# The first operations of a fused attention and channel-mix kernel: inputs on other queues, w_phi in one DMA, k's first transposes ahead of q

## The chip, the cores and the metric

One core of one Trainium2 chip. The metric is the device time of one execution in microseconds (us). The kernel before took 284.57, 334.05 and 285.87 us in three runs; the median is 285.87. A profile comes from one execution, and its times count from the first instruction of the program, the start of the span.

## The reference

The input is q, k and v of shape (8, 8, 576, 64) (batch, heads, sequence, head dimension), a feature matrix `w_phi` (64 x 128), and the parameters of a channel mix. First an attention with a feature map, then the mix on its output:

```python
def phi(x):
    proj = np.einsum('bhsd,df->bhsf', x, w_phi)
    proj = proj - np.max(np.abs(proj), axis=-1, keepdims=True)
    return np.concatenate([np.exp(proj), np.exp(-proj)], axis=-1)
q_p, k_p = (phi(q), phi(k))
kv = np.einsum('bhsf,bhsd->bhfd', k_p, v)
num = np.einsum('bhsf,bhfd->bhsd', q_p, kv)
den = np.einsum('bhsf,bhf->bhs', q_p, np.sum(k_p, axis=2))[..., None] + 1e-06
x = (num / den)                      # heads side by side: (8, 576, 512)
...
xk = mu_k * x + (1.0 - mu_k) * x_prev     # x_prev: x one position earlier
xr = mu_r * x + (1.0 - mu_r) * x_prev
k = np.maximum(xk @ w_k, 0.0)
v = k * k @ w_v
out = 1.0 / (1.0 + np.exp(-(xr @ w_r))) * v
```

Inputs and the output are float32; matrix products run on bfloat16 operands.

## The kernel before

Work is cut into 32 pairs of heads (8 batches of 4 pairs). Within a pair, 128 partitions hold two heads of 64 partitions, and each partition has nine positions of 64 values: 576 columns of k, then 576 of q, in the tile `nat` (1152 columns, nine groups of 128). Groups 0 to 3 are k alone, group 4 is the last 64 columns of k and the first 64 of q, groups 5 to 8 are q alone. For the first two batches TensorE transposes these groups (`pt`, L331 to L339, with the identity `ident`), ScalarE or VectorE copies them from PSUM to the tile `qkT` (`pa` and `pb`, L341 to L347); later batches are transposed by DMA.

Per pair n the operations are, by the names that the order uses:

- `ptn.0`, `ptn.1`: two runs of transposes, and `pan`, `pbn`: their copies. `trn` is only a name for both.
- `kpn`, `qpn` (L571, L574): projections of k (groups 0 to 3) and q (groups 5 to 8) with `wph` (w_phi in bf16, on both halves of the partitions). `tp` (L457) does group 4, the odd position.
- `rkn`, `rqn` (L577, L582): VectorE's maxima of absolute values; `rt` (L470) for group 4.
- `ean`, `ebn` (L602): ScalarE's exponentials of k; `em`, `eme`, `ekt` smaller ones.
- `mh`, `mt`, `mc`, and `mhe`, `mte`, `mce` for group 4: the maxima of q are split into two bf16 parts on GpSimd, transposed and copied. `qt` and `qa`, `qb` then form the exponentials of q transposed (L626, L639).
- `va`, `vb` (L595): v scaled on GpSimd. `kv`, `kc`, `nd`, `ra`, `rd`: products, division.
- `xt`, `xe`, `xf`, `df`, `xa`, `xb`: the mix; `h`, `rl`, `sq`, `r`, `th`, `v`, `ob`, `so`: the channel mix itself.

Nothing schedules this at run time. `plan.op(...)` registers each operation as a function, and the string `ORDER` (L19) is the order in which all of them are issued, written out. In `name/ENGINE` the engine is chosen, in `name:i` the PSUM buffer, and `+n@i` puts n filler matmuls of the tile `ones` (L285) ahead of the operation; their product is not used. Each engine runs its instructions in this order, and an instruction waits for the semaphores of the tiles that it touches. The costs and dependences that `op` is given are not used by `order()`.

What starts the kernel:

- `hk` (L358) loads k of pair 0 as float32 on the SP queue, `hq` (L362) q on the ACT queue, each 128 partitions of 2304 bytes. `lk0.0.d` (VectorE) and `lq0.0.d` (ScalarE) cast them into `nat`.
- `wphi` (L244) loads w_phi in two DMAs of 64 partitions on SP; `dve1` (L251) casts it to `wph`.
- `mus` (L442) loads the mix factors `mu_k_t` and `mu_r_t` on SP, element by element.
- `lk`, `lq` (L317) load and cast the other pairs through the GpSimd (POOL) queue, `lv` (L324) loads v on POOL or SP, `wk`, `wr`, `wv` (L431) the weights on POOL.
- `ident` (L248) makes the identity on GpSimd, `ones`, `dve2`, `dve3` (L254 to L272) set constants on VectorE: zeroed tiles, a column of `xs`, ones in `tq`, the bf16 identity, and a selection matrix `sel`.

Of the kernel before, what the change touches and what calls it, by code (L numbers as in the profile page):

```python
# [16 lines left out]


ORDER = """  # L19
ones hk hq ident dve2 hk.d hq.d wphi wphi.d lk0.1 lk0.1.d lq0.1 lq0.1.d mus mus.d lk0.2 lk0.2.d dve3  # L20
lq0.2 lq0.2.d lv0.0/POOL lv0.0.d lk0.0.d/DVE lq0.0.d/ACT lv0.1/SP lv0.1.d pt0.0:0+9@0 lv0.2/SP
lv0.2.d pt0.1:1 pa0/DVE pb0/ACT tr0 dve1 tp0.0:0+1@2 kp0:1 rt0.0 qp0:2 rk0 eme0.0 mhe0.0/POOL ekt0.0
pt1.0:1+1@0 lk1.0 lk1.0.d pa1/ACT mte0.0:0 rq0 ea0 lq1.0 lq1.0.d pt1.1:1+2@2 pb1/DVE tr1 lk1.2
lk1.2.d eb0 kp1:2+2@2 tp0.1:0 lq1.2 lq1.2.d rt0.1 em0 rk1 qp1:1+1@1 ekt0.1 mh0/POOL eme0.1 wk.0
wk.0.d mt0:1+1@1 mc0/ACT mce0.0/DVE rq1 ea1 qt0:0+1@2 wk.1 wk.1.d wk.d pt2.0:1 qa0 pt2.1:0
mhe0.1/DVE mh1/POOL pa2/DVE pb2/DVE tr2 eb1 vb0/POOL pt3.0:1+2@3 pt3.1:0 pa3/DVE qb0 pb3/DVE tr3
va0/POOL mte0.1:1+1@3 qp2:2 mt1:0 rq2 qp3:1 mce0.1/ACT mc1/ACT em1 qte0.1:1 wr.0 wr.0.d qt1:0 eqe0.1
qte0.0:0 rq3 lv1.0/POOL lv1.0.d qa1 tp0.2:2 va1/POOL qb1 rt0.2 kp2:1+3@1 rk2 vb1/POOL ekt0.2
# [103 lines left out]
class Plan:  # L132
# [6 lines left out]
    def op(self, name, eng, w, at, fn, deps=(), alloc=(), rel=(), chain=None, mode=0, port=False, alt=()):  # L139
        assert name not in self.ops, name  # L140
        self.ops[name] = dict(name=name, fn=fn, alloc=alloc, alt=alt)
# [19 lines left out]
def kernel(  # L161
# [80 lines left out]
    mu_r_t = consts.tile([128, NDC], FP, name="mu_r_t")  # L242

    def c_wphi():  # L244
        for hh in range(2):
            nc.sync.dma_start(out=wph_f32[64 * hh:64 * hh + 64, :], in_=w_phi)

    def c_ident():  # L248
        make_identity(nc, ident_f32)
# [4 lines left out]
    def c_ones():  # L254
        nc.vector.memset(ones, 1.0)

    def c_dve2():
        for t in mhls + mhlts + [zero]:
            nc.vector.memset(t, 0.0)
        for t in xss:  # L260
            nc.vector.memset(t[:, :, 0:1], 0.0)
        for t in tqs[0] + tqs[1]:
            nc.vector.memset(t[:, :, 0:64], 1.0)

    def c_dve3():
        nc.vector.tensor_copy(ident, ident_f32)
        for i in range(2):
            iv = ident_f32[:, 64 * i:64 * i + 16].rearrange("p (k l g) -> p k l g", k=2, l=2)
            nc.vector.tensor_tensor(sel3[:, i, :].rearrange("p (k g) -> p k g", k=2),
                                    iv[:, :, 0, :], iv[:, :, 1, :], op=ALU.add)  # L270
        nc.vector.tensor_tensor(sel3[:, 2, :], sel3[:, 0, :], sel3[:, 1, :], op=ALU.add)
        nc.vector.tensor_copy(sel, sel3[:, 2, :].to_broadcast([128, 8, 128]))  # L272

    op("wphi", "SP", 1.2, -98, c_wphi, ["hk"])
    op("wphi.d", "DMA", 0.1, -98, None, ["wphi"])
    op("ident", "POOL", 1.1, -99, c_ident)
    op("ones", "DVE", 0.3, -10, c_ones)
    op("dve1", "DVE", 0.2, -9, c_dve1, ["wphi.d", "dve2"])
    op("dve2", "DVE", 1.9, -8, c_dve2, ["ones"])
    op("dve3", "DVE", 1.3, -7, c_dve3, ["ident", "dve2"])  # L280

    st = {}
# [29 lines left out]
    def add_load(b, a0, a1, at, first):  # L312
        al = lambda t: [(t, (t, b))] if first else []
        n = a1 - a0
        tag = f"{b}.{a0}"

        def ld(which):  # L317
            def f():
                t = get(nat, b, inp, [128, NP, 2 * X], BF, "nat")
                src, o = ((k, 0), (q, X))[which]  # L320
                nc.gpsimd.dma_start(out=t[:, a0:a1, o:o + X], in_=heads(src, b, a0, a1))
            return f

        def ldv(c0, c1):  # L324
            def f(eng):
                t = get(vt, (b, c0 // 2), inp, [128, 2, X], FP, "vt", bufs=BUFS["vt"])
                (nc.sync if eng == "SP" else nc.gpsimd).dma_start(out=t[:, c0 % 2:c0 % 2 + c1 - c0, :],
                                                                  in_=heads(v, b, c0, c1))
            return f

        def pt(b, a, bk):  # L331
            def f():
                i = NP * b + a
                get(qkT, b, inp, [128, NP * R, 128], BF, "qkT")
                ps = motile(("mo", f"pt{i}.{bk}"), "ps_pt")
                st["pb", i, bk] = pb = ps.bitcast(BF).rearrange("p (g t) -> p g t", t=128)
                for g in range(5 * bk, min(R, 5 * bk + 5)):
                    nc.tensor.transpose(pb[:, g - 5 * bk, :], nat[b][:, a, g * 128:(g + 1) * 128], ident)
            return f  # L339

        def pc(b, a, bk):  # L341
            def f(eng):
                t = qkT[b]
                n_ = 5 - bk
                o = t[:, R * a + 5 * bk:R * a + 5 * bk + n_, :]
                copy(eng, o, st["pb", NP * b + a, bk][:, 0:n_, :])
            return f  # L347

        def tr(p0, p1):
            def f():  # L350
                t = get(qkT, b, inp, [128, NP * R, 128], BF, "qkT")
                nc.sync.dma_start_transpose(out=t[:, R * p0:R * p1, :],
                                            in_=nat[b][:, p0:p1, :].rearrange("p a x -> p (a x)"))
            return f

        g = 0.95 * n
        if b == 0 and a0 == 0:
            def hk():  # L358
                st["kq"] = mm.tile([128, NFC, 512], BF, name="kk").rearrange("p a x -> p (a x)").bitcast(FP)[:, 0:2 * X].rearrange("p (i x) -> p i x", i=2)
                nc.sync.dma_start(out=st["kq"][:, 0, :], in_=heads(k, 0, 0, 1)[:, 0, :])  # L360

            def hq():  # L362
                nc.scalar.dma_start(out=st["kq"][:, 1, :], in_=heads(q, 0, 0, 1)[:, 0, :])

            def ck(i):
                def f(eng):
                    t = get(nat, b, inp, [128, NP, 2 * X], BF, "nat")
                    o = t[:, 0, i * X:(i + 1) * X]
                    copy(eng, o, st["kq"][:, i, :])
                return f  # L370

            op("hk", "SP", 0.6, -99, hk)
            op("hk.d", "DMA", g, -99, None, ["hk", "dve2"])
            op("hq", "ACT", 0.6, -99, hq, ["hk"])
            op("hq.d", "DMA", g, -99, None, ["hq", "dve2"])
            op(f"lk{tag}.d", "DVE", 0.4, -90, ck(0), ["hk.d"], alloc=al("nat"), alt=("DVE", "ACT"))
            op(f"lq{tag}.d", "ACT", 0.65, -90, ck(1), ["hq.d", f"lk{tag}.d"], alt=("ACT", "DVE"))
        else:
            op(f"lk{tag}", "POOL", 0.75, at("lk"), ld(0), ["ident"], alloc=al("nat"), chain="ld")
            op(f"lk{tag}.d", "DMA", g, at("lk"), None, [f"lk{tag}"])  # L380
            op(f"lq{tag}", "POOL", 0.75, at("lq"), ld(1), [f"lk{tag}"], chain="ld")
            op(f"lq{tag}.d", "DMA", g, at("lq"), None, [f"lq{tag}"])
        for c0 in range(a0, a1, 2):
            c1 = min(c0 + 2, a1)
            vn = f"lv{b}.{c0}"
            op(vn, "POOL", 0.75, at("lv"), ldv(c0, c1), ["ident"], chain="lv", alt=("POOL", "SP"),
               alloc=[("vt", ("vt", (b, c0 // 2)))] if c0 % 2 == 0 else [])
            op(vn + ".d", "DMA", g, at("lv"), None, [vn])
        if b < NPT:
            for a in range(a0, a1):  # L390
                i = NP * b + a
                for bk in range(2):
                    op(f"pt{i}.{bk}", "PE", 0.3, ("pt", i), pt(b, a, bk), [f"lk{tag}.d", f"lq{tag}.d", "dve3"],
                       alloc=[("mo", ("mo", f"pt{i}.{bk}"))] + (al("qkT") if a == a0 and bk == 0 else []), rel=[("nat", b)],
                       chain="pt")
                    op(f"{'pa' if bk == 0 else 'pb'}{i}", "DVE", 0.48, ("pa", i), pc(b, a, bk), [f"pt{i}.{bk}"],
                       rel=[("mo", f"pt{i}.{bk}")], alt=("DVE", "ACT"))
                op(f"tr{i}", "NONE", 0, 0, None, [f"pa{i}", f"pb{i}"])
        else:
            for p0 in range(a0, a1, 2):  # L400
                tg = f"tr{b}.{p0}"
                op(tg, "SP", 2.8, at("tr"), tr(p0, p0 + 2), [f"lk{tag}.d", f"lq{tag}.d"], chain="tr",
                   alloc=al("qkT") if p0 == a0 else [])
                op(tg + ".d", "DMA", 2, at("tr"), None, [tg], rel=[("nat", b)])
                for a in range(p0, p0 + 2):
                    op(f"tr{NP * b + a}", "NONE", 0, 0, None, [tg + ".d"])
# [35 lines left out]
    def mus():  # L442
        nc.sync.dma_start(out=mu_k_t, in_=moe_mu_k.rearrange("(c p) -> p c", p=128))
        nc.sync.dma_start(out=mu_r_t, in_=moe_mu_r.rearrange("(c p) -> p c", p=128))

    op("mus", "SP", 1.2, -3, mus, ["wphi"])
    op("mus.d", "DMA", 0.3, -3, None, ["mus"])

# [568 lines left out]
```

## Time and profile before

| | |
|---|---|
| median of three runs | 285.87 us |
| span of the profiled execution | 275.3 us |
| its records ahead of the span | 10.8 us, so about 286.1 us in all |
| first DMAs of k and q: issue to landing | 3.9 and 4.1 us |
| the two of w_phi | 3.8 and 4.4 us |
| mu_k, mu_r | 7.1 and 8.5 us |
| three parts of v of batch 0 | 8.0, 8.6 and 9.8 us |
| filler matmuls ahead of the first transposes | 9, 4.02 us |
| first transposes start | 5.53 us |
| first projection of k starts | 7.01 us |
| second pair's first exponential of k starts | 12.03 us |

How to read it: a row of the timeline gives start, duration, engine, line, operation, output<-inputs, shapes, a count when several are merged, and in brackets the idle time of the engine before it and what ended that. PE is TensorE, PEld its weight loads, DVE VectorE, ACT ScalarE, POOL GpSimd, SP the queue of SyncE; a q behind a name means the sequencer, as when it issues a DMA. An operation's reported end lies some 0.1 us behind the start of the next one on the same engine, so a chain is summed from start to start. The packet records of the trace give queue, size, start and duration of each DMA packet.

### The profile page before, as it was taken

Reading aid. Unit: us, or ns where it says so; the run is one execution under the profiler, and the core shown is the slowest. Engines: PE = TensorE matmul, PEld = TensorE weight load, DVE = VectorE, ACT = ScalarE, POOL = GpSimd, SP = SyncE. Lnnn points to the kernel's source line nnn. Section 1 sums busy time; section 2 is a strip of 40 time slices with the busy share of each in tenths; the row PEclk is TensorE's granted clock in tenths of the full one; section 3 lists DMA queues with packets and bytes.
Section 4 is the critical chain, followed back from the end, with each engine's and each line's share of the span. In section 5 each row is a group of like instructions: output and inputs, shape, how many; then the busy total and the mean of one; then the engine's idle time right before and its main releaser. Section 6 shows DMA issues by size and latency. Waiting matters only on the chain.

```text
span 275.3 us, 8865 instructions
## 1 busy us (share of the span) xinstructions
PE 261.7 (95%) x3682; PEld 154.1 (56%) x3730; DVE 234.6 (85%) x388; ACT 223.1 (81%) x413; POOL 142.4 (52%) x193
## 2 busy tenths in 40 slices
PE   7899889999899999999999999999999999999993
PEld 3567656566555566555565666555566565444542
DVE  6999999999799989999999889998889897864222
ACT  3899999999899997899898999789987777616330
POOL 5799557976818682633459465821931611300200
PEclk9999999999999999999999999999999999999999
DMA  7999999599999899759699998981725324142134
GB/s 147 285 209 250 209 213 174 114 235 175 238 129 200 202 219 185 155 127 248 99 166 164 215 249 142 171 255 41 161 89 88 77 52 100 42 110 67 29 88 116
DMA packets 65817, 42.89 MB, mean 156 GB/s; under 512 B 47152, under 2 KB 57008, under 8 KB 65776
## 3 DMA queue, kind: packets, MB, share of 16 engines
q1 hardware_dynamic: 54496, 27.54, 49.3%
q0 software_dynamic: 11056, 14.42, 29.1%
q8 instruction: 29, 0.48, 0.8%
q10 hardware_dynamic: 224, 0.36, 0.5%
q14 instruction: 12, 0.10, 0.1%
HBM read 33.62 MB, written 9.44 MB: 156 GB/s over the span
## 4 chain that ended last, share of the span: by engine, by line
PE 75%; DVE 8%; ACT 6%; issue 4%; DMA 3%; POOL 2%; SPq 0%; POOLq 0%; ACTq 0%
PE ps_h L810 19%; PE ps_v L843 17%; PE ps_r L829 9%; PE ps_nd L677 5%; PE ps_kv L656 5%; DMA qkT<-nat 3%; PE ps_he L897 3%; PE ps_ve L929 3%; PE ps_k L566 2%; PE ps_qT L630 2%; PE ps_q L566 2%; PE ps_qT L636 2%; ACT k L605 2%; DVE nmk L579 2%; PE ps_f L292 1%
## 5 line engine op out<-in xcount | busy, mean ns | idle before, releaser
L597 POOL TENSOR_TENSOR v<-vt,v 128x576 bf16<-128x576 f32 x59 | 69.8, 1203 | 33.5 <-ACT v L591 31.1
L605 ACT ACTIVATE k<-ps_k 128x1024 bf16<-128x1024 f32 x64 | 64.8, 1047 | 1.3 <-DVE nmk L579 1.3
L643 ACT ACTIVATE q<-ps_qT 128x1024 bf16<-128x1024 f32 x64 | 63.8, 1054 | 1.8 <-PE ps_qT L636 1.7
L810 PE MATMUL ps_h<-xk,wk_bf 128*128 128x512 bf16 x235 | 60.5, 380 | 1.2
L843 PE MATMUL ps_v<-wv_bf,kk 128*128 128x512 bf16 x244 | 58.2, 379 | 0.6
L579 DVE TENSOR_REDUCE nmk<-ps_k 128x8 f32<-128x1024 f32 x32 | 38.8, 1217 | 1.8 <-PE ps_k L566 1.5
L584 DVE TENSOR_REDUCE nmq<-ps_q 128x8 f32<-128x1024 f32 x32 | 38.3, 1217 | 1.6 <-PE ps_q L566 1.4
L843 PEld LDWEIGHTS <-kk 128*128 128x128 bf16 x256 | 24.1, 98 | 27.3
L810 PEld LDWEIGHTS <-wk_bf 128*128 128x128 bf16 x256 | 22.7, 97 | 25.0 <-issue 0.7
L206 ACT ACTIVATE krelu<-ps_h 128x512 bf16<-128x512 f32 x48 | 28.8, 611 | 9.3 <-PE ps_h L810 9.3
L726 POOL TENSOR_TENSOR diff<-xs 128x576 bf16<-128x576 bf16 x15 | 20.2, 1346 | 28.8 <-ACT xs L706 12.7
L214 POOL TENSOR_TENSOR kk<-krelu 128x512 bf16<-128x512 bf16 x18 | 19.1, 1068 | 30.3 <-ACT krelu L206 26.6
L849 DVE SCALAR_TENSOR_TENSOR ob<-rt,ps_v 128x512 f32<-128x512 bf16 x32 | 21.7, 682 | 14.3 <-PE ps_v L843 12.7
L829 PE MATMUL ps_r<-wr_bf,xr 128*128 128x512 bf16 x116 | 31.1, 380 | 0.7
L835 ACT ACTIVATE rt<-ps_r 128x512 bf16<-128x512 f32 x32 | 19.7, 615 | 8.8 <-PE ps_r L829 8.7
L732 DVE SCALAR_TENSOR_TENSOR xk<-diff,mu_k_t,xs 128x576 bf16<-128x576 bf16 x32 | 26.7, 839 | 0.1
L689 DVE TENSOR_TENSOR x_sc<-ps_nd,rden 128x640 bf16<-128x640 f32 x32 | 26.0, 817 | 0.6
L732 DVE SCALAR_TENSOR_TENSOR xr<-diff,mu_r_t,xs 128x576 bf16<-128x576 bf16 x32 | 25.6, 806 | 0.1
L656 PE MATMUL ps_kv<-v,k 64*128 64x65 bf16 x1024 | 22.4, 190 | 0.5 <-ACT q L643 0.2
L566 PEld LDWEIGHTS <-qkT 64*128 64x128 bf16 x512 | 16.5, 94 | 11.0 <-issue 8.0
L656 PEld LDWEIGHTS <-k 64*128 64x128 bf16 x1024 | 19.3, 94 | 5.7 <-issue 1.8
L677 PE MATMUL ps_nd<-kv,q 128*128 128x65 bf16 x512 | 21.4, 193 | 0.0
(102 smaller groups left out, 414.3 us busy)
## 6 DMA issues: line engine op xcount, KB each, us to landing
out_dram<-ob SPq DMA_DIRECT2D x70, 128.0 KB, 2.5
vt<-in_v_dram SPq DMA_DIRECT2D x11, 576.0 KB, 6.1
nat<-in_k_dram POOLq DMA_DIRECT2D x6, 576.0 KB, 7.8
nat<-in_q_dram POOLq DMA_DIRECT2D x6, 576.0 KB, 8.0
vt<-in_v_dram POOLq DMA_DIRECT2D x4, 576.0 KB, 6.0
wk_bf<-in_moe_w_k_dram POOLq DMA_DIRECT2D x2, 512.0 KB, 11.4
wv_bf<-in_moe_w_v_dram POOLq DMA_DIRECT2D x2, 512.0 KB, 10.6
nat<-in_k_dram POOLq DMA_DIRECT2D x3, 288.0 KB, 6.9
```

What stands on the lines that cost most here:

```text
L206: nc.scalar.activation(out_, in_, AF.Relu, scale=HALF)
L579: nc.vector.tensor_reduce(t[:, j, :], s["k"].rearrange("p a (g f) -> p (a g) f", f=128), axis=AX.X, op=ALU.max, apply_absolute_value=True, ...
L584: nc.vector.tensor_reduce(t[:, j, :], s["q"].rearrange("p a (g f) -> p (a g) f", f=128), axis=AX.X, op=ALU.max, apply_absolute_value=True, ...
L597: (nc.vector if eng == "DVE" else nc.gpsimd).tensor_tensor(vb[:, a, pn, :, 0:64], vt[b, a // 2][:, a % 2, :].rearrange("p (s d) -> p s d", ...
L605: nc.scalar.activation(s[f"k{pn}"], s["k"].rearrange("p a (g f) -> p (a g) f", f=128), AF.Exp, scale=(1.0 if pn == 0 else -1.0))
L643: nc.scalar.activation(t.rearrange("f x (a p) -> f x a p", a=2), s["qT"].rearrange("f a (x p) -> f x a p", p=64), AF.Exp, scale=(1.0 if pn ...
L656: nc.tensor.matmul(ps[:, hh, pn * 65:(pn + 1) * 65], lhsT=s[f"k{pn}"][r, c, :], rhs=vb[r, a, pn, 2 * g + par, :], start=(pn == 0 and c == ...
L677: nc.tensor.matmul(ps[:, bk, o * 65:(o + 1) * 65], lhsT=tail if sl < 2 else s[f"q{pn}"][:, 2 * G + h, :], rhs=s["kv"][:, h, pn, :], start= ...
L732: nc.vector.scalar_tensor_tensor(out=t[:, a, (b % 2) * S:(b % 2 + 1) * S], in0=s["d"], scalar=mu[:, a:a + 1], in1=xs[:, a, 0:S], op0=ALU.m ...
L810: nc.tensor.matmul(ps, lhsT=wk_bf[:, c, fc * 128:(fc + 1) * 128], rhs=xkt[bp][:, c, m0:m0 + 512], start=(c == 0), stop=(c == NDC - 1))
L829: nc.tensor.matmul(ps, lhsT=xrt[bp][:, c, m0 + ci * 128:m0 + (ci + 1) * 128], rhs=wr_bf[:, c, :], start=(c == 0), stop=(c == NDC - 1))
L843: nc.tensor.matmul(ps, lhsT=s["kk"][:, fc, ci * 128:(ci + 1) * 128], rhs=wv_bf[:, fc, :], start=(fc == 0), stop=(fc == NFC - 1))
```

## The change

The first operations are issued in another order and on other queues; from `wk.1` on the order is the same string as before.

- q of pair 0 is issued on SP right behind k; w_phi is one DMA on ACT, whose source is the matrix read twice.
- A pair's nine transposes are cut 4+5 instead of 5+4, for all pairs that TensorE transposes.
- The constants: the cast of the identity (`dve0`) comes first, then the zeroed tiles (`dve2`), then `dve3`; the column of `xs` and the ones in `tq` are set on GpSimd (`dve4`).
- On VectorE the cast of w_phi (`dve1`) comes ahead of the copy `pa0`; on TensorE `kp0` comes ahead of `pt0.1`, with `pt1.0`, `tp0.0` and `qp0` behind. On ScalarE: q's cast, `pb0`, `pa1`, `ea0`, `ekt0.0`, `eb0`, `eme0.0`.
- On GpSimd `mh0` comes ahead of the loads `lk1.2` and `lq1.2`. Behind these stands `muz`, which zeroes `mu_k_t`; the DMAs of the mix factors wait for it, and `lv0.2` follows them on SP. `lv0.1` moves from SP to POOL.
- Eight filler matmuls stand ahead of `wk.1` instead of 17.

```diff
-ones hk hq ident dve2 hk.d hq.d wphi wphi.d lk0.1 lk0.1.d lq0.1 lq0.1.d mus mus.d lk0.2 lk0.2.d dve3
-lq0.2 lq0.2.d lv0.0/POOL lv0.0.d lk0.0.d/DVE lq0.0.d/ACT lv0.1/SP lv0.1.d pt0.0:0+9@0 lv0.2/SP
-lv0.2.d pt0.1:1 pa0/DVE pb0/ACT tr0 dve1 tp0.0:0+1@2 kp0:1 rt0.0 qp0:2 rk0 eme0.0 mhe0.0/POOL ekt0.0
-pt1.0:1+1@0 lk1.0 lk1.0.d pa1/ACT mte0.0:0 rq0 ea0 lq1.0 lq1.0.d pt1.1:1+2@2 pb1/DVE tr1 lk1.2
-lk1.2.d eb0 kp1:2+2@2 tp0.1:0 lq1.2 lq1.2.d rt0.1 em0 rk1 qp1:1+1@1 ekt0.1 mh0/POOL eme0.1 wk.0
-wk.0.d mt0:1+1@1 mc0/ACT mce0.0/DVE rq1 ea1 qt0:0+1@2 wk.1 wk.1.d wk.d pt2.0:1 qa0 pt2.1:0
+ones hk hk.d wphi wphi.d hq hq.d ident dve0 lk0.1 lk0.1.d dve2 lq0.1 lq0.1.d lk0.2 lk0.2.d dve3
+lq0.2 lq0.2.d lv0.0/POOL lv0.0.d lv0.1/POOL lv0.1.d lk0.0.d/DVE pt0.0:0+5@0 dve4 lq0.0.d/ACT dve1
+pa0/DVE kp0:1+1@2 pt0.1:1 rk0 pb0/ACT pt1.0:0 tr0 tp0.0:0 rt0.0 qp0:2 pa1/ACT mhe0.0/POOL rq0 ea0
+pt1.1:1+1@0 lk1.0 lk1.0.d ekt0.0 pb1/DVE tr1 mte0.0:0 lq1.0 lq1.0.d kp1:2 tp0.1:0 eb0 rt0.1
+mh0/POOL eme0.0 rk1 qp1:1+1@1 lk1.2 lk1.2.d mt0:1 mc0/ACT em0 lq1.2 lq1.2.d mce0.0/DVE muz mus mus.d
+lv0.2/SP lv0.2.d rq1 ekt0.1 wk.0 wk.0.d eme0.1 ea1 qt0:0+1@2 wk.1 wk.1.d wk.d pt2.0:1 qa0 pt2.1:0
...
     def c_wphi():
-        for hh in range(2):
-            nc.sync.dma_start(out=wph_f32[64 * hh:64 * hh + 64, :], in_=w_phi)
+        twice = bass.AP(w_phi.tensor, w_phi.offset, [[0, 2]] + [list(x) for x in w_phi.ap])
+        nc.scalar.dma_start(out=wph_f32, in_=twice)
...
+    def c_dve0():
+        nc.vector.tensor_copy(ident, ident_f32)
+
     def c_dve2():
         for t in mhls + mhlts + [zero]:
             nc.vector.memset(t, 0.0)
+
+    def c_dve4():
         for t in xss:
-            nc.vector.memset(t[:, :, 0:1], 0.0)
+            nc.gpsimd.memset(t[:, :, 0:1], 0.0)
         for t in tqs[0] + tqs[1]:
-            nc.vector.memset(t[:, :, 0:64], 1.0)
+            nc.gpsimd.memset(t[:, :, 0:64], 1.0)
...
-                for g in range(5 * bk, min(R, 5 * bk + 5)):
-                    nc.tensor.transpose(pb[:, g - 5 * bk, :], nat[b][:, a, g * 128:(g + 1) * 128], ident)
+                for g in ((0, 1, 2, 3), (4, 5, 6, 7, 8))[bk]:
+                    nc.tensor.transpose(pb[:, g - 4 * bk, :], nat[b][:, a, g * 128:(g + 1) * 128], ident)
...
-                n_ = 5 - bk
-                o = t[:, R * a + 5 * bk:R * a + 5 * bk + n_, :]
+                n_ = 4 + bk
+                o = t[:, R * a + 4 * bk:R * a + 4 * bk + n_, :]
...
-                nc.scalar.dma_start(out=st["kq"][:, 1, :], in_=heads(q, 0, 0, 1)[:, 0, :])
+                nc.sync.dma_start(out=st["kq"][:, 1, :], in_=heads(q, 0, 0, 1)[:, 0, :])
...
+    def muz():
+        nc.gpsimd.memset(mu_k_t, 0.0)
+
+    op("muz", "POOL", 0.1, -3, muz)
```

More of the change, by code (lines that the diff above doesn't have):

```diff
@@ L259, in c_dve2 @@
             nc.vector.memset(t, 0.0)
+    def c_dve4():
         for t in xss:
-            nc.vector.memset(t[:, :, 0:1], 0.0)
+            nc.gpsimd.memset(t[:, :, 0:1], 0.0)
         for t in tqs[0] + tqs[1]:
-            nc.vector.memset(t[:, :, 0:64], 1.0)
+            nc.gpsimd.memset(t[:, :, 0:64], 1.0)
     def c_dve3():
-        nc.vector.tensor_copy(ident, ident_f32)
         for i in range(2):
@@ L272, in c_dve3 @@
         nc.vector.tensor_copy(sel, sel3[:, 2, :].to_broadcast([128, 8, 128]))
-    op("wphi", "SP", 1.2, -98, c_wphi, ["hk"])
+    op("wphi", "ACT", 0.6, -98, c_wphi)
     op("wphi.d", "DMA", 0.1, -98, None, ["wphi"])
@@ L278 @@
     op("dve1", "DVE", 0.2, -9, c_dve1, ["wphi.d", "dve2"])
+    op("dve0", "DVE", 0.2, -8, c_dve0, ["ident"])
+    op("dve4", "POOL", 1.5, -8, c_dve4)
     op("dve2", "DVE", 1.9, -8, c_dve2, ["ones"])
@@ L373, in add_load @@
             op("hk.d", "DMA", g, -99, None, ["hk", "dve2"])
-            op("hq", "ACT", 0.6, -99, hq, ["hk"])
+            op("hq", "SP", 0.6, -99, hq, ["hk"])
             op("hq.d", "DMA", g, -99, None, ["hq", "dve2"])
```

## The prediction

> **What bounds the kernel now.** I read the page first. One core, no throttled stretch, and three engines that are nearly full over the whole span:
>
> ```profile
> span 275.3 us, 8865 instructions
> PE 261.7 (95%) x3682; PEld 154.1 (56%) x3730; DVE 234.6 (85%) x388; ACT 223.1 (81%) x413; POOL 142.4 (52%) x193
> ```
>
> The trace's records start 10.8 us before the span (packets of the launch), so this execution took about 286.1 us; the median of the three runs, 285.87, is 0.2 below it. A shift of the start adds to either one for one, if nothing later has slack. The chain that ended last shows whether it has: it begins in the prologue and passes through DVE, then ACT, without a wait for a DMA.
>
> ```profile
> 1.46 4.03 PE ps_f L292 x9
> 5.49 0.04 issue
> 5.53 0.70 PE ps_pt L338 x5
> ...
> 6.67 0.23 DVE wph L252
> ...
> 7.64 1.13 DVE nmk L579
> 8.77 1.14 DVE nmq L584
> ```
>
> To be seen: nine filler matmuls carry the chain to 5.49, then pair 0's transposes, the copy of the transposed k, the cast of w_phi, and DVE's reductions. After 12 us ACT and DVE have no gaps to give back; the table of windows says so (columns: window, its length, then PE, PEld, DVE, ACT, POOL busy, clock, DMA share, GB/s):
>
> ```profile
> 7.00:10.00 3.00, 2.58 (x34) 1.58 (x37) 2.79 (x4) 2.46 (x8) 2.21 (x5) 1.00 1.35 228
> 20.00:30.00 10.00, 9.26 (x228) 7.55 (x227) 9.94 (x19) 9.99 (x23) 9.66 (x16) 1.00 1.17 239
> ```
>
> The second thing in it: a DMA share above 1 means that packets overlap; the DMA engines are full from 4 us on. The timeline gives the first inputs (start, duration):
>
> ```profile
> 1.21 1.22 SPq L246 DMA_DIRECT2D wph_f<-in_w_phi_dram  x2
> 4.67 0.46 DVE L202 CAST nat<-kk 128x576 bf16<-128x576 f32 x1 [0.62 <-DMA kk<-in_k_dram]
> 4.83 0.67 ACT L200 CAST nat<-kk 128x576 bf16<-128x576 f32 x1 [2.37 <-DMA kk<-in_q_dram]
> 7.01 0.39 PE L566 MATMUL ps_k<-wph,qkT 64*128 64x128 bf16 x8
> 12.03 1.03 ACT L605 ACTIVATE k<-ps_k 128x1024 bf16<-128x1024 f32 x1
> ```
>
> k lands at 4.65, q at 4.81, w_phi's halves at 4.98 and 6.28 (its issues plus 3.8 and 4.4 from its tile's view), used at 6.67. The order after `wk.1` is the same in both kernels, so I compare when ACT starts pair 1's first exponential (12.03): from there ACT is gapless to 18.6.
>
> **What the Trainium skill says.** "DMA: Bandwidth & Descriptors", section "Why a DMA increments its semaphore by 16 and not by 1": an SP or ACT DMA is spread over the largest k up to 16 that divides the slowest dimension of both sides; its rules for authors name a leading zero-stride broadcast of c copies as confined to c engines. The new w_phi source is exactly that: 2 copies x 64 rows x 128. So two engines, 64 packets of 512 B each, where before each half had 4 on each of 16. No transfer in this trace has such a shape. Same page, "Queues, rings and completion order": an engine goes round its queues packet by packet. The trace agrees roughly: mu_k (issued 2.47, 7.1 to landing) and mu_r (3.10, 8.5) land 2.0 us apart for 33 packets per engine, 61 ns each although one takes 9; between two of them stands one 106 ns packet of POOL's queue. "TensorE: Matmul & The Clock Gate", Part 1: the array runs at half clock until it was busy for some 3.4 us. Agrees: nine fillers took 4.02 us, 0.43 each; two later ones at 8.35 took 0.59 against 0.38 for one, 0.21 each.
>
> **The change, part by part.**
>
> 1. *q behind k on SP.* Packet records: 2304 B take 93 ns on an engine, 8 each for k and q. k and q together end at 4.0 to 4.2, landings 0.6 later. k alone first should end about 1 us earlier: k lands near 3.7 (from the v load at 46.21, whose first 128 packets took 1.23 us alone: 1.8+1.3+0.6), q near 4.9. ACT's q cast is then no later than before by more than 0.1.
> 2. *First transposes of k alone, 4+5 instead of 5+4.* Nine transposes as before. The copies swap sizes (DVE 0.41 and 0.49, ACT 0.59 and 0.69); where the halves of a pair sit on different engines (pairs 0, 1, 5, 7) plus and minus 0.1 cancel. The first projection of k no longer waits for q: with k at 3.7, its cast ends at 4.2, four transposes at 4.9.
> 3. *Nine fillers fewer* (8 for 17): the first five end at 1.46+5x0.43 = 3.6, before k's cast, so none stands on the path any more; worth 0.35 (5.53 against 5.18) alone.
> 4. *Memsets to POOL.* DVE loses xs (0.08) and tq (1.09); it ends its constants near 3.2 instead of 4.05, which k at 3.7 needs. On POOL, between 1.1 us (DVE's) and 1.8 (by its 0.20 for a 128x128 f32 memset); POOL idles 2.95 us before `mhe0.0`, which covers that and the 0.56 of one more v issue. Cost 0; without that cover about 1 us on `mhe0.0`, then `lk1.0`, behind it.
> 5. *mu behind a POOL memset, v late.* mu moves from 2.47 past POOL's `lq1.2`; its first user is at 31.66. v's third part follows on SP; rival C.
> 6. *w_phi, the price that decides.* DVE's order is cast k, cast w_phi (waits for its landing, L), copy of the transposed k; PE's is four transposes, a filler, `kp0`, then `pt0.1`. So the late w_phi holds `kp0`, and behind it q's transposes and everything else, and on DVE the copy.
>
> L: each of the two engines serves 64x27 ns = 1.73 us of w_phi and 16x93 ns = 1.49 of k and q from 2.0 on. Lower end: 2.0+1.73+1.49+0.6 = 5.8, if POOL's packets take no turn. But these (106 ns) start at 3.86 and don't stop. Until then, after a slow start to 2.3, about 13 rounds of 93+27 ns: 13 of 64 done. The other 51 at two per POOL packet, as mu had it, cost 27+53 = 80 ns each, 4.1 us; with the rest of q (0.3) and the landing (0.6): 3.9+4.1+0.9 = 8.9. One for one, 133 ns each: 11.5, the upper end. I take **L = 8.9**.
>
> From L on, with start-to-start times of the timeline: w_phi cast and copy 0.6, `kp0` at L+0.6 (9.5, before 7.01), `rk0` L+1.05 to 2.2. `pt0.1` behind `kp0` done at L+1.3, its copy on ACT 0.65 to L+2.0, `tp0.0` to 2.3, `rt0.0` to 2.65, `rq0` to 3.8. POOL: `mhe0.0` to L+3.1, two load issues (1.47) to 4.6, `mh0` to 5.0, transpose to 5.3. ACT from L+2.0: copy 0.5, `ea0` 0.9, `ekt0.0` 0.39, `eb0` 0.9, `eme0.0` 0.2 to 4.9, waits for 5.3, then 0.16+0.24+0.34+0.2: pair 1's exponential at L+6.3 = 15.2, against 12.03: **+3.2**. PE has meanwhile stood idle from about 5 to 9.5, so `kp0`, five transposes, `tp0.0` and `qp0` (0.9 us of issue) run at half clock: between 0 and +0.9, I take +0.4. Sum **+3.6**: 286.1 to 289.7 for the profiled execution, 285.9 to **289.5** at the median. Behind it DVE and ACT are full, so nothing gives it back.
>
> **Rivals.**
>
> A, the forecast (0.58): w_phi lands between 7.5 and 11.5, 287.7 to 292.5.
>
> A0 (0.13): two engines, but small packets hardly wait; L = 5.8 to 7.5. The shift is L-5.7: at 5.8 it is +0.1, 286.0. For: half of the packets may go before POOL's start. Against: w_phi's second half took until 6.28 in the run before with only 4 packets an engine.
>
> B, faster (0.24): the transfer is spread over 16 engines after all, 8 packets each, nothing ahead of them on ACT's queue, landing near 4.4, no later than k's cast. It decides from L below 5.7. Then `kp0` at 5.35, `pt0.1` behind it done at 6.4, copy to 7.1, `rt0.0` 7.4 to 7.75, `rq0` to 8.9; POOL's `mh0` ends at 10.1, pair 1's exponential starts at 11.35: 0.7 gained there, 0.9 on DVE (`rq0` 7.75 against 8.68). 0.8 less: 285.1. More is not there, since q's cast, copy and `tp0.0` follow in line.
>
> C, v late (0.05): v's third part now follows mu, at about L+6.6 = 15.5; before, mu's first issue to that landing took 11.6 (2.47 to 14.03), with 1.2 of another v part between. It lands at about 25.9; POOL wants it at 23.50+3.6 = 27.1, and PE has another 1.75 (25.8 to 27.55). Only some 3 us more of queueing make a stall; with 4 more, +1: 290.5.
>
> **How the numbers follow.** The likeliest is A at 289.5, its own range 287.7 to 292. A0 gives 286 to 287.7, B 284.6 to 285.6. Leaving out some 8% at each end: 284.7 to 292. A measurement of this kernel tells about 2% (5.7 us) from no change: above 291.6 takes L over about 11.0, a fifth of A: 0.12. Below 280.2 no case reaches: 0.01. The rest, 0.87, is within.
>
> **What would show it.** Right: the cast of w_phi on DVE idles for its DMA, 4 to 5 us, with issue to landing near 8; `kp0` near 9.5; fillers few, PE idle before it; ACT's exponential of pair 1 near 15.5; the rest shifted alike. Wrong: w_phi's issue to landing under 5 us means rival B; an idle before `va2` for v on POOL means C; `kp0` late but the span unchanged means slack that I don't see.

## The result, and the profile after

The changed kernel took 293.69 us at the median of six runs (290.85 to 298.24); the kernel before took 284.74 beside it (six runs, 278.77 to 334.05). The ratio is 1.050 with a 95% interval of 1.039 to 1.061: slower, and above the range. (A ratio compares the runs of each kernel within 1.5% of its fastest; since the kernel before scatters widely, it can differ from the quotient of the medians.) The profiled execution took 296.35 us, the second longest of the six; 294.6 of it are span.

First the page: its span, the busy time of each engine, and the clock by slices of 7.4 us.

```profile
span 294.6 us, 8847 instructions
PE 265.5 (90%) x3674; PEld 157.3 (53%) x3721; DVE 235.4 (80%) x382; ACT 223.7 (76%) x413; POOL 143.7 (49%) x201
PEclk9999779999975999999999999999999999999999
```

The work is the same within 4 us on every engine; the span is 19.3 longer. So the engines wait, and the clock line says where to look: two places, at about 30 to 40 and 84 to 94 us, where TensorE had been idle and then ran at half clock. (The clock records of this execution begin 12.5 us into the span, so the line says nothing of the clock before; the lengths of the matmuls do.) The windows name the same places (columns as before):

```profile
20.00:30.00 10.00, 8.60 (x207) 6.91 (x202) 9.89 (x19) 10.00 (x24) 5.06 (x11) 1.00 1.18 252
30.00:40.00 10.00, 5.89 (x107) 4.56 (x107) 4.33 (x7) 3.94 (x9) 7.70 (x9) 0.66 1.16 188
80.00:90.00 10.00, 1.54 (x43) 1.45 (x44) 1.10 (x1) 0.35 (x2) 1.06 (x1) 0.71 1.35 183
```

DVE and ACT, the full engines of before, are busy 4.3 and 3.9 of the ten microseconds from 30 on, and hardly at all from 80 to 90. The chain of waits over the first 40 us (start, length, what) has two transfers in it where the one of before had none:

```profile
0.74 5.18 DMA wph_f<-in_w_phi_dram
...
5.94 0.96 DVE wph L252
...
6.98 0.61 PE ps_k L576 x8
7.59 0.66 PE ps_pt L344 x5
...
14.29 1.55 SPq L450
...
15.88 15.75 DMA vt<-in_v_dram
...
31.77 2.30 POOL v L607 x2
```

w_phi stands at the start, as forecast, but lands at 5.92 and not at 8.9; its cast on DVE runs to 6.90, over four times as long as before, which is taken up below. Then the chain goes over POOL's loads to the mix factors on SP (mu_r, L450) and to v's third part, queued behind them: 15.75 us. A third transfer stands in the chain of the whole span:

```profile
72.26 16.16 DMA qkT<-nat
```

(the chain of before had the same transfer in it, 7.78 us from 63.81), and TensorE's waits give the price of the last two (in total, times, longest):

```profile
PE ps_e L476 <- DMA qkT<-nat: 9.4, 1, 9.4
PE ps_kv L666 <- POOL v L607: 5.0, 1, 5.0
```

The rows of the timeline that answer to those shown of before:

```profile
0.74 1.16 ACTq L246 DMA_DIRECT2D wph_f<-in_w_phi_dram  x1
...
3.63 0.51 DVE L202 CAST nat<-kk 128x576 bf16<-128x576 f32 x1 [0.60 <-DMA kk<-in_k_dram]
...
6.98 0.61 PE L576 MATMUL ps_k<-wph,qkT 64*128 64x128 bf16 x8 [1.75 <-DVE qkT L202]
...
13.83 1.03 ACT L615 ACTIVATE k<-ps_k 128x1024 bf16<-128x1024 f32 x1
...
31.77 2.29 POOL L607 TENSOR_TENSOR v<-vt,v 128x576 bf16<-128x576 f32 x2 [6.43 <-DMA vt<-in_v_dram]
```

Against before, pair 1's first exponential is 1.80 later (13.83 for 12.03), and the scaling of v's third part 8.27 later (31.77 for 23.50). From there on the shift holds until TensorE's wait for `qkT`: 9.4 us where before had 1.1, plus 10 us at half clock behind it, which bring it to the 19.3 of the end. So three things to test: the start (1.8), v behind the mix factors (6.5), and the wait for `qkT` (about 8 in the wait, 3 behind it).

### The profile page after: what moved, and what is told of

It is laid out like the page before. It is cut to its first block, busy times and chain, and to the rows that moved or that the text cites. A ratio compares the mean times of both kernels' runs of the same rounds, so it can differ in the third digit from the quotient of the medians.

```text
span 294.6 us, 8847 instructions
## 1 busy us (share of the span) xinstructions
PE 265.5 (90%) x3674; PEld 157.3 (53%) x3721; DVE 235.4 (80%) x382; ACT 223.7 (76%) x413; POOL 143.7 (49%) x201
## 4 chain that ended last, share of the span: by engine, by line
PE 70%; DMA 13%; DVE 5%; POOL 4%; issue 4%; ACT 2%; SPq 1%; POOLq 0%
PE ps_h L820 18%; PE ps_v L853 16%; PE ps_r L839 9%; DMA qkT<-nat 5%; DMA vt<-in_v_dram 5%; PE ps_nd L687 5%; PE ps_kv L666 5%; PE ps_he L907 3%; PE ps_k L576 2%; PE ps_ve L939 2%; POOL v L607 2%; PE ps_qT L640 2%; DMA wph_f<-in_w_phi_dram 2%; PE ps_q L576 2%; PE ps_qT L646 2%
## 5 line engine op out<-in xcount | busy, mean ns | idle before, releaser
L839 PE MATMUL ps_r<-wr_bf,xr 128*128 128x512 bf16 x116 | 31.8, 386 | 0.9 <-issue 0.2
L666 PE MATMUL ps_kv<-v,k 64*128 64x65 bf16 x1024 | 23.4, 194 | 5.5 <-POOL v L607 5.0
L666 PEld LDWEIGHTS <-k 64*128 64x128 bf16 x1024 | 20.3, 96 | 10.7 <-issue 7.2
L576 PEld LDWEIGHTS <-qkT 64*128 64x128 bf16 x512 | 17.3, 97 | 13.4 <-issue 8.3
```

Source lines behind the costliest of these rows:

```text
L576: nc.tensor.matmul(ps[:, par, g * 128:(g + 1) * 128], lhsT=qkT[b][r, g0 + gg + g, :], rhs=wph[r, :], start=(g == 0), stop=(g == 3))
L666: nc.tensor.matmul(ps[:, hh, pn * 65:(pn + 1) * 65], lhsT=s[f"k{pn}"][r, c, :], rhs=vb[r, a, pn, 2 * g + par, :], start=(pn == 0 and c == ...
L839: nc.tensor.matmul(ps, lhsT=xrt[bp][:, c, m0 + ci * 128:m0 + (ci + 1) * 128], rhs=wr_bf[:, c, :], start=(c == 0), stop=(c == NDC - 1))
```

## The experiments

The kernel before again, for a second profile:

> The kernel before once more, for a second profile. Its first profile has a span of 275.3 us, some 6 to 8 us shorter than its own typical time less 1.75 us. Theory P (the typical execution of both kernels holds a wait for a transposing DMA near the end of the first third, which the first profile of before happened to miss): span 281 to 284, and TensorE waits for the tile qkT from a DMA for 5 us or more somewhere between 60 and 100 us. Theory N (that wait belongs to the changed kernel alone): no wait for such a DMA over 2 us in it, whatever the span.

One run: 278.62 us, span 276.8, wait for `qkT` 1.6 us. The wait of over 5 us that the expectation wanted wasn't there, but the run was also near the low end: 37 runs of the kernel before, taken later beside other kernels, spread from 277.15 to 289.45. What sets that spread was open at this point. The run settles one thing: time and span differ by 1.8 us (and by as much for the changed kernel), not by the 10.8 of the prediction. The profiled execution of before thus took about 277.1 us.

**The start and v, by undoing them.** Three kernels, each the changed one with parts put back.

```diff
 e1_wphi16, w_phi over 16 engines again, still on ACT
-        twice = ...
-        nc.scalar.dma_start(out=wph_f32, in_=twice)
+        for hh in range(2):
+            nc.scalar.dma_start(out=wph_f32[64 * hh:64 * hh + 64, :], in_=w_phi)
 e2_vfirst, v's third part ahead of the mix factors at the same place
-muz mus mus.d lv0.2/SP lv0.2.d
+muz lv0.2/SP lv0.2.d mus mus.d     (muz also sets a column of v's tile, so v waits there too)
 e3_both: both edits
```

> The changed kernel with w_phi in two DMAs of 64 partitions on ACT in place of the one with a doubled source. Theory W (two engines serve w_phi, it lands at 5.92, and the half-clock TensorE behind it costs the rest of the 1.8 us by which pair 1's exponential is late): w_phi lands by 4.6, the first projection of k starts near 5.4 in place of 6.98, pair 1's exponential at 11.3 to 12.2 in place of 13.83, and 1.5 to 2.5 us less than the changed kernel at the end if v's third part is then not later; if that part is still the bound, the gain is 0 to 1 us at the end, since v moves with the GpSimd queue by as much. Rival (w_phi's shape does not matter): 13.8 stays.

> The changed kernel with v's third part issued ahead of the mix factors on SP, at the same time (a GpSimd memset of a column of its tile holds it back as the factors are held). Theory V (v queues behind the factors' 4-byte packets, 64 on each engine, each of which waits for a packet of GpSimd's queue): v issued near 13.9 lands by 22, GpSimd does not wait for it, the scaling starts near 25.4 in place of 31.77, and the end is about 6 us sooner than the changed kernel, ratio to before near 1.01. Rival (v is late because it is issued 12 us later into full DMA engines): it lands after 26 all the same, and the ratio stays above 1.03.

> Both edits. Theories W and V together: pair 1's exponential at 11.3 to 12.2, no wait for v, and the end at 0 to 1 us below before, ratio 0.99 to 1.00. If something else in the change costs time (the wait for the transposed qkT, fewer fillers), the ratio stays above 1.01 with both early marks repaired.

Every ratio in the tables is to runs of the kernel before taken beside that group. Their medians were 282.82 us (19 runs) for e, 279.38 (8) for f and 281.87 (37) for g. The last table repeats the changed kernel's ratio from above.

| | median us (runs) | ratio to before, 95% | w_phi cast | pair 1 exponential | v's third part scaled | POOL waits for v | wait for `qkT` |
|---|---|---|---|---|---|---|---|
| e1_wphi16 | 285.70 (6) | 1.020 [1.010, 1.031] | 5.18 | 12.72 | 30.77 | 6.64 | 1.3 |
| e2_vfirst | 285.19 (14) | 1.005 [0.998, 1.012] | 5.92 | 13.98 | 26.01 | none | 3.4 |
| e3_both | 285.87 (6) | 1.013 [0.998, 1.028] | 5.76 | 13.98 | 25.56 | none | 4.6 |

With v ahead of the mix factors the wait for v is gone, and v lands 9.65 us after its issue (13.82 to 23.47) instead of 15.75. The same row as above, now of e2_vfirst:

```profile
26.01 2.29 POOL L608 TENSOR_TENSOR v<-vt,v 128x576 bf16<-128x576 f32 x2 [0.17 <-ACT v L602]
```

The start fell out less clean. w_phi over 16 engines gains 1.1 us in e1_wphi16 (12.72, w_phi landed at 5.08), but nothing in e3_both (13.98, landed at 5.66). In both, TensorE is at half clock: `kp0` takes 0.61 us where before took 0.39, and in e3_both the fillers are at half speed until after 14. The timeline of TensorE in e3_both (a filler takes some 0.6 at half clock and 0.38 at full, as the one at 17.66 does):

```profile
1.46 2.31 PE L298 MATMUL ps_f<-ones 128*128 128x512 bf16 x5 [1.46 <-DVE ones L255]
...
6.98 0.61 PE L577 MATMUL ps_k<-wph,qkT 64*128 64x128 bf16 x8 [1.75 <-DVE qkT L202]
...
13.97 0.59 PE L298 MATMUL ps_g<-ones 128*128 128x512 bf16 x1 [0.89 <-ACT tk L510]
```

So the fillers that the change took away were a suspect of their own.

There is a second one. `kp0` starts at 6.98 in e3_both as in the changed kernel, though w_phi landed 0.26 us sooner. It waits for DVE's copy, and DVE works while POOL sets the ones in `tq`, which the change moved there. The rows of the changed kernel, then those of e3_both:

```profile
5.72 1.10 POOL L268 MEMSET tq<- 128x256 bf16 x4
5.94 0.96 DVE L252 CAST wph<-wph_f 128x128 bf16<-128x128 f32 x1 [1.80 <-DMA wph_f<-in_w_phi_dram]
6.08 0.82 DVE L202 COPY qkT<-ps_pt 128x512 bf16<-128x512 bf16 x1
...
5.76 1.14 DVE L252 CAST wph<-wph_f 128x128 bf16<-128x128 f32 x1 [1.62 <-DMA wph_f<-in_w_phi_dram]
5.90 1.00 DVE L202 COPY qkT<-ps_pt 128x512 bf16<-128x512 bf16 x1
```

The cast took 0.22 us in before, and the copy takes 0.42 in e1_wphi16. Here both last until 6.90, just behind the end of the memsets at 6.82. It is the same in all six profiles in which the cast starts between 5.76 and 6.12 (the changed kernel, e2, e3, and f2, g1, g2 below): wherever it starts, it ends at 6.90 and `kp0` starts at 6.97 or 6.98. Where w_phi lands by 5.1 (e1, and f3 and g4 below), the copy is over by 5.75. So w_phi was late enough to run into the memsets, and their end seems to set `kp0`. No run moves them back to DVE or to a later place, so this is argued and not shown. It would explain why w_phi over 16 engines gained nothing in e3_both.

**Each suspect alone, and the fillers.** Four kernels: the kernel before with the mix factors and v moved as in the change, and nothing else; the changed kernel with v ahead and fillers put back, without and with w_phi over 16 engines; and the kernel before with w_phi as one DMA at its old place.

```diff
 f1_before_vlate (on the kernel before)
-lq0.1.d mus mus.d lk0.2 ... lv0.1/SP lv0.1.d pt0.0:0+9@0 lv0.2/SP lv0.2.d
+lq0.1.d lk0.2 ... lv0.1/POOL lv0.1.d ... pt0.0:0+9@0
-mh0/POOL eme0.1
+mh0/POOL muz mus mus.d lv0.2/SP lv0.2.d eme0.1
 f2_vfirst_fill (on e2_vfirst), f3_both_fill (on e3_both)
-pt0.0:0+5@0 ... kp0:1+1@2
+pt0.0:0+6@0 ... kp0:1+3@2
 f4_before_wphi2 (on the kernel before)
-        for hh in range(2):
-            nc.sync.dma_start(out=wph_f32[64 * hh:64 * hh + 64, :], in_=w_phi)
+        twice = ...
+        nc.sync.dma_start(out=wph_f32, in_=twice)
```

> The kernel before, with only the mix factors and v moved as the change moves them: the second part of v to GpSimd's queue, the factors held by a GpSimd memset, v's third part behind them on SP. Theory V (v waits behind the factors' small packets): that part issued near 13 lands near 29 to 31, GpSimd waits for it some 5 to 7 us, pair 1's exponential stays at 12.0, and the end is 5 to 7 us later than before, ratio 1.018 to 1.026. Rival (the late start of the changed kernel makes the wait, since the factors are issued later then): less than 3 us of wait here.

> The changed kernel with v ahead of the factors, and three more filler matmuls: six ahead of the first transposes and three ahead of the first projection of k, where TensorE otherwise idles for w_phi. w_phi stays on two engines. Theory H (the half clock until 12 to 18 us costs most of what is still lost at the start): clock full by 8.5, the first projection of k still near 7.0, pair 1's exponential at 12.4 to 13.0 in place of 13.98, the next of q at 13.4 to 14.2 in place of 15.68, shift at 25 us 1.0 or less in place of 3.4. Rival (the order with the projection ahead of q's transposes is the loss): the exponential of pair 1 stays above 13.6 with a full clock.

> As before it, with w_phi in two DMAs on 16 engines too. Theories W, V and H together: w_phi lands at 5.1 to 5.7, pair 1's exponential at 11.5 to 12.3, no wait for v, shift against before between -0.7 and +0.5 at 25 us, end within 1 us of before if the later waits for the transposed qkT are alike.

> The kernel before with only w_phi's two DMAs on SP replaced by the one with the doubled source, at the same place behind k. Theory W: two engines; it lands between 6.5 and 8.5 (before: 6.28 and 5.6), the cast of w_phi waits up to 1.8 us for it, and pair 1's exponential moves by as much. Rival (the packets of 512 B pass the others quickly, and the engines hardly matter): it lands by 6.3 and the exponential stays at 12.0 to 12.2.

| | median us (runs) | ratio to before, 95% | w_phi cast | pair 1 exponential | v's third part scaled | wait for `qkT` |
|---|---|---|---|---|---|---|
| f1_before_vlate | 287.92 (4) | 1.037 [1.028, 1.045] | 6.28 | 11.64 | 28.50 | 3.9 |
| f2_vfirst_fill | 284.57 (4) | 1.028 [1.017, 1.039] | 6.12 | 12.88 | 24.84 | 4.4 |
| f3_both_fill | 285.22 (4) | none given | 4.76 | 12.18 | 24.14 | 1.2 |
| f4_before_wphi2 | 279.51 (1) | one run | 6.88 | 12.29 | 23.72 | 2.9 |

f1_before_vlate shows v alone, with the first operations in before's order (its 11.64 is even 0.39 earlier). Its timeline, SP's issues and then POOL's wait:

```profile
11.20 0.40 SPq L443 DMA_DIRECT2D mu_k_t<-in_moe_mu_k_dram  x1
11.64 0.56 SPq L444 DMA_DIRECT2D mu_r_t<-in_moe_mu_r_dram  x1
12.25 0.70 SPq L327 DMA_DIRECT2D vt<-in_v_dram  x1
...
28.50 2.29 POOL L601 TENSOR_TENSOR v<-vt,v 128x576 bf16<-128x576 f32 x2 [5.42 <-DMA vt<-in_v_dram]
```

v lands 16.1 us after its issue, POOL waits 5.4, and the scaling is 5.0 later than before. So that part of the change costs 5 us even with the start of before; in the changed kernel, putting v ahead gained 5.8 (31.77 to 26.01 in e2_vfirst).

The fillers show in the pair f2_vfirst_fill and e2_vfirst: 1.10 us (12.88 against 13.98), with w_phi as late in both; TensorE is at full clock at `kp0` (0.40). And f2 against f3 shows what the two-engine transfer costs in this order with these fillers: 0.70 us (12.88 against 12.18), with what it meets of the memsets, which f3's cast at 4.76 escaped. In the old order it costs nothing that stands out (f4_before_wphi2: 12.29, against 12.03, 12.14 and 12.27 in three profiles of that start). The medians of f1, f2 and f3 still lie 5.8, 6.1 and 7.5 us above the 277.1 of before's profiled execution plus their shift at v's scaling (5.0, 1.3, 0.6). In the profiles of f1 and f2 the wait for `qkT`, 2.8 and 3.3 longer than before's, and half clock behind it (3.4 and 6.8 us long) stand in that place; f3's profile, of its quick run of 278.75, has neither, and its slower runs have no profile.

**The wait for `qkT`.** It belongs to the DMA that transposes pairs 14 and 15 (`tr3.2`, on SP). It was there in every profile so far, between 1.1 and 9.4 us, in the kernel before too. What the profiles have in common: within 0.8 us of its issue, GpSimd issues the load of batch 4's k (`lk4.0`), a meeting that nothing in the order prevents. So I moved that one load behind the next scaling of v, in the changed kernel and in the kernel before, and, in a last kernel, on top of all repairs.

```diff
 g2_after_lklate (changed kernel), g3_before_lklate (kernel before)
-rk11 ea10 lk4.0 lk4.0.d v0.1:0 ... ob0.0 va10/POOL nd8:0
+rk11 ea10 v0.1:0 ... ob0.0 va10/POOL lk4.0 lk4.0.d nd8:0
 g4_all_lklate (on e3_both): the same, and
-pt0.0:0+5@0 ... kp0:1+1@2
+pt0.0:0+6@0 ... kp0:1+2@2
 g1_after_again: the changed kernel once more
```

> The changed kernel once more, for a second profile. Theory S (start): pair 1's first exponential near 13.8, v's third part landing near 31 and GpSimd waiting 6 to 7 us for it are there again, since they follow from the order of the queues. Theory T (the long wait of TensorE for the DMA-transposed qkT of pairs 14 and 15, 9.4 us in the first profile) is chance in size: between 1 and 10 us, landing 8 to 16 us after issue. Rival: it is 9 to 10 us again, a fixed property of the changed order.

> The changed kernel with one load moved: k of batch 4 (lk4.0) is issued behind va10 on GpSimd instead of ahead of it, some 3 to 4 us later, so that it no longer starts in the same microsecond as the transposing DMA of qkT for pairs 14 and 15. Theory: the two share the engines and slow each other; then that DMA lands within 6 to 8 us of its issue, TensorE waits under 1 us for qkT, and the kernel's span is near 284 (the start's and v's 8 us stay), a median some 285 to 287. Rival: the transposes are slow whatever runs beside them; then the wait stays 1 to 10 us and the median stays near 293.

> The kernel before with the same load moved behind va10. If the meeting of the load and the transposing DMA makes the scatter of the kernel before (277 to 290), then its times gather at 275 to 278 and the median is 1 to 2% lower: ratio 0.98 to 0.99; the wait of TensorE for qkT, 1.1 to 1.6 in the two profiles of before, goes to nearly nothing. Rival: no difference, ratio 0.995 to 1.005, the scatter stays.

> The changed kernel with all that was found put right: w_phi as two DMAs over 16 engines, v's third part ahead of the mix factors, 6 fillers ahead of the first transposes and 2 ahead of kp0 (5 and 1 in the change), and lk4.0 behind va10. Pair 1's first exponential near 12.0 (before 12.03), no wait of GpSimd for v, no wait for qkT: a span of 274 to 276 and a median near 276 to 277, ratio 0.975 to 0.99. Rival: the wait for qkT stays, and it is at 281 to 286.

| | median us (runs, range) | ratio to before, 95% | span | pair 1 exponential | v's third part scaled | `tr3.2` issue to landing | wait for `qkT` |
|---|---|---|---|---|---|---|---|
| before | 281.87 (37, 277.15 to 289.45) | 1 | 275.3 | 12.03 | 23.50 | 7.8 | 1.1 |
| changed | 293.69 (6, 290.85 to 298.24) | 1.050 [1.039, 1.061] | 294.6 | 13.83 | 31.77 | 16.2 | 9.4 |
| g1_after_again | 285.75 (1) | one run | 284.0 | 13.98 | 32.17 | 7.8 | 0.8 |
| g2_after_lklate | 286.31 (4, 285.45 to 287.19) | 1.020 [1.014, 1.027] | 284.4 | 13.99 | 31.83 | 5.5 | none |
| g3_before_lklate | 278.04 (16, 277.56 to 284.63) | 0.991 [0.988, 0.994] | 276.3 | 12.27 | 23.71 | 5.4 | none |
| g4_all_lklate | 278.97 (22, 277.75 to 281.80) | 0.999 [0.997, 1.002] | 276.0 | 11.72 | 23.68 | 5.2 | none |

g1 has the start and v's wait again to within 0.5 us and no long wait for `qkT`: that wait is not a fixed property of the change. g2 and g3 show what it depends on. One load moved, and the wait is gone from both profiles, the scatter from most runs: 14 of the 16 of g3 lie between 277.56 and 278.58, where 5 of 37 of the kernel before lie below 279. The timeline of g3, SP's transposes (two, 61.46 and 64.36) and POOL's loads:

```profile
61.46 6.41 SPq L352 DMA_TRANSPOSE qkT<-nat  x2
...
67.62 1.51 POOL L597 TENSOR_TENSOR v<-vt,v 128x576 bf16<-128x576 f32 x1 [3.03 <-ACT v L591]
69.08 0.79 POOL L321 DMA_DIRECT2D nat<-in_k_dram  x1
```

In the kernel before the load stood at 64.30, and the second transpose, issued from 63.81 on, met its packets. It now has the DMA engines to itself until it has all but landed, at 69.7.

With that noise gone, the change can be read: g2 against g3, the two orders alike but for the change, 286.31 against 278.04 at the median and 284.4 against 276.3 in span, 8.3 and 8.1 us. The shift at v's scaling is 8.1 too (31.83 against 23.71). So the change costs 8.1 to 8.3 us: 1.7 at the start, the other 6.4 behind the mix factors, nothing that shows after it.

g4 has the order of the change with its three faults mended. Its first exponential is 0.55 earlier than g3's and its v on time, but the median is 0.9 above g3's, not below: the half microsecond did not reach the end, and why is not shown.

## Why the prediction was wrong

The direction was right, and the case forecast ("two engines, w_phi late, `kp0` held and everything behind it") is in part what the start shows. The main failure is the queueing time of v behind the mix factors, mis-sized so that a rival at 0.05 was the main event. The start was mis-sized too, with errors that partly cancelled, and one thing later in the kernel was left out.

1. *Where the time went: rival C, "v late".* It had mechanism and place right and the size wrong: "It lands at about 25.9; POOL wants it at 23.50+3.6 = 27.1". It landed at 31.63, and POOL stood ready at 25.3 (31.77 less 6.43). The failed term is the 10.4 us from mu's issue to v's landing, which took 17.8 (13.85 to 31.63). It was taken from the kernel before, where the mix factors ran beside k and q loads of 1152-byte packets, two of theirs to one of POOL's, 61 ns each. At the new place POOL's queue holds the weights. Packets started in each microsecond, counted over the 16 engines in the packet records of the changed kernel:

```
us     mix factors (4 B)   POOL, weights (2048 B)   POOL (1024 B)   v (2304 B)
20         95                    93                      0              0
22        102                   100                      0              0
23        103                   103                      0              0
25        164                     5                    118              0
28          2                     0                     72             85
30          8                     0                    174             21
```

(A few of the 4-byte packets end other transfers.) From 20 to 24 us the two queues go in nearly equal numbers, so that a turn costs on average one POOL packet of 172 ns; before's took 106, for two turns. The 64 packets that the two factors put on each engine took from 18.5 to 26.5 us, 125 ns apiece, and v's 16 per engine came only then. That is 8.0 us where 61 ns apiece make 3.9, so 4.1 of the 7.4 us by which the term was short. The rest lies around it: 4.25 us pass from the factors' issue to the first of their packets at 18.1, and v needs 5.1 from its first packet (26.53) to its landing. The first of these is not a matter of small packets: with v ahead, in e2_vfirst, its own first packet comes 4.07 us after its issue. What holds it back is not shown. The Trainium skill, "DMA: Bandwidth & Descriptors", section "Queues, rings and completion order", says that an engine takes its queues in turn, packet by packet: for the factors the counts agree, and it means that four bytes wait as long for their turn as two thousand. I had written that down for mu_k and mu_r and not carried it to the queue that they would meet later.

2. *L, "the price that decides".* The two engines were right: w_phi's transfer ends with two 4-byte packets (5.43 and 5.56 us), where e1's two DMAs end with 32, and "Why a DMA increments its semaphore by 16 and not by 1", on the same page, has each engine that takes part send one increment. Its one issue took 1.16 us, each of before's two 0.59. But L was 5.92 and not 8.9. By the packet records both halves of its working failed. By POOL's first packet at 3.66, 48 of the 128 had started, 24 an engine where I had 13 ("about 13 rounds of 93+27 ns"): 24 in 0.6 us leave no room for a turn of k or q after each. And of "the other 51 at two per POOL packet" only 16 of 128 started between 3.7 and 4.6; from 4.6 on the last 64 started within 0.94 us, one every 29 ns on each engine. So this transfer did not take turns throughout as the mix factors did. Why is not shown. L = 5.92 lies in rival A0, which gives a shift of 0.2.

3. *The sum behind L.* It was given as L+6.3 and measured as L+7.9 (13.83 less 5.92). The parts, by the chain: the cast of w_phi and the copy behind it run to 6.90, beside POOL's memsets, so `kp0` starts at L+1.06 and not at L+0.6; `kp0` and q's five transposes end at L+2.3 and not at L+1.3; `tp0.0` to `mhe0.0` add 0.3, and the transpose of `mh0` 0.4 behind `qp1`. The first of these touches a term that was put at nothing, the memsets on POOL ("Cost 0"): it looked at what they delay on POOL and not at DVE beside them. If the copy had its usual 0.42 us, it would end some 0.4 sooner (an estimate from 6.08 and 6.90). The half clock was in the sum, at 0.4, as a consequence of a late w_phi. It was a consequence of the fillers: "none stands on the path any more" is true and misses what they are for. With 5 ahead of the transposes and 1 ahead of `kp0` the array is at half clock until 11.5 to 20.1 us in all six profiles; with 6 and 2 or 3, full speed comes between 4.1 and 6.7, and f2 gained 1.10 by it. The Trainium skill, "TensorE: Matmul & The Clock Gate", Part 1, puts the warm-up at a busy window of some 3.4 us that runs freely, so that the moment varies. Here full clock comes 2.7 us after the first filler in f2 and g4 (1.46 to 4.2 and 4.1) and 5.2 after it in f3, which has the same six ahead of the transposes; the window's length shows in the half-clock stretches behind idle TensorE, 6.83 and 10.24 us in the clock records of the changed kernel, two and three times 3.41. How dense the busy time must be no run here shows. In sum, L came 3.0 us sooner than forecast and the sum behind it was 1.6 longer, so that pair 1's exponential moved by 1.8 us, of 3.2 forecast and 3.6 with the clock: two errors, and it was luck that they pulled against each other.

4. *What lay later.* "Behind it DVE and ACT are full, so nothing gives it back": nothing was given back, but something was added. A wait of 1.1 us for `qkT` at 71 us stands in the profile of before, a few lines below the ones that I used, and in the profiles it varies by up to 8.6 us, with half clock behind the longer ones. The chain of before, read as "without a wait for a DMA", holds the transpose behind it for 7.78 us. The wait is in the kernel before's scatter as well, so it isn't the change's own. It makes up the other part of the 19.3 in the profile, and the six runs of the changed kernel lie 4 to 12 above g2.

5. *The base.* "The trace's records start 10.8 us before the span, so this execution took about 286.1": it took about 277.1 (span plus 1.8). The match with the median of 285.87 was chance; the profiled execution was one of the quick ones of a wide scatter. The wrong base hid that scatter.

Right were: k's landing (3.60, forecast 3.7) and q's (5.16, forecast 4.9); that the memsets delay nothing on POOL itself (it still idles 3.03 us before `mhe0.0`); the swap of halves; and that the start moves everything behind it alike. Rival B (0.7 sooner at the start, 11.35) shows in part, in g4's 11.72; but f1, with before's order, has 11.64, and at the end of g4 nothing is left of it.

Open: what holds the first packet on SP back for some 4 us, and whether the memsets, moved, would give back their part. Open too: how large a meeting of the load and the transposes turns out. Eleven profiles with it have landings from 7.7 to 16.2 us, and the order of the two issues (the load from 0.42 ahead to 0.72 behind) doesn't rank them. Whether the changed kernel meets it worse than the kernel before, as six runs 4 to 12 us above g2 suggest and g1 at 0.6 below it does not, is not settled either.

## What to carry to other kernels

A transfer of single elements is small in bytes and long in turns: count its packets per engine, times the packet of whatever queue runs beside it at the new place, and keep a transfer with a due time ahead of it, not behind. Work moved to an idle engine may still hold the one it came from: look at what runs beside it at its new time. Fillers that no longer bound the chain may still carry the clock, so price them by what follows at half speed. And when a kernel's times scatter by 4%, find the wait in the profile that varies before pricing a change of 1%: here one load moved by 4 us took most of the scatter away.

## What the runs showed of the hardware

- A one-element load of 64 packets an engine took 125 ns a packet in the mean, beside POOL packets of mostly 1024 and 2048 bytes (96 and 172 ns). A transfer of 2304-byte packets behind it landed 15.75 to 17.2 us after its issue (five profiles); ahead of it, 8.8 to 9.8 (five).
- w_phi on two engines, 64 packets of 512 bytes each, landed 5.18 us after its issue, at 5.92. Over 16 engines its second half landed between 4.66 and 5.66 (e1, e3, f3, g4). So an eighth of the engines came 0.3 to 1.3 us later.
- A cast on DVE that takes 0.22 us alone took 0.78 to 1.14 while POOL ran memsets of 1.10 us, and ended at 6.90 us in six profiles, whenever it had started.
- TensorE with five fillers ahead of its first transposes and one behind stayed at half clock until 11.5 to 20.1 us (six profiles); with six and two or three, or with before's nine, until 4.1 to 6.7 (eight profiles).
- A DMA transpose that landed in 5.2 to 5.5 us alone took 7.7 to 16.2 when a POOL load of 1152-byte packets was issued within 0.8 us of it. In the worst case both slowed: from 76 to 78 us its 256-byte packets took 206 ns each (19 at 72 to 74), and the load's 209 (107 elsewhere).
